# Buffer order in SBUF, column counts of the experts' last groups, and the place of the gate's sums in a fused attention and expert kernel

## The chip, the cores and the metric

The kernel runs on one core of a Trainium2 chip. The metric is the device time of one launch in microseconds; a comparison goes by the median of several runs. The profile is that of one further execution.

## What is computed

Three layers follow each other. Chunked attention works on 8 x 8 heads, 576 rows of 64, in chunks of 64 rows (softmax of q k^T / 8, times v); its output, 4608 tokens of 512, goes through a dense block, x = g @ w_out with h = x @ w_in and g = h - tanh(h) (512 to 2048 to 512). Then a router chooses two of eight experts for each token:

```python
logits = x @ w_gate
noise_scale = np.log1p(np.exp(x @ w_noise))
noisy_logits = logits + noise_scale * noise
top2 = np.argpartition(-noisy_logits, 2, axis=1)[:, :2]
...
h = np.maximum(x[mask] @ w1[e], 0.0)
out[mask] += top2_w[mask, k, None] * (h @ w2[e])
```

Each expert has 512 to 1024 to 512. With the inputs that the reference draws, the eight experts get 1106, 1152, 1151, 1148, 1239, 1151, 1109 and 1160 tokens; these counts come from running the reference's own arithmetic, and the kernel knows them only at run time.

## The kernel before

All products of the dense block and of the experts are made from split float32 numbers: each operand has a high and a low part, and three of the four products of parts are summed (`PASSES`), so a product over 512 inputs is 12 matmuls (3 passes by 4 blocks of 128). A *step* is one block of 128 hidden units: `products1` (L331) makes 12 matmuls into a PSUM bank `hp`, with the weights as the stationary 128 x 128 operand and the tokens (tile `xt0` or `xt1`) as the moving one; `activate` has ScalarE and VectorE turn `hp` into two parts in `gt`; `products2` (L439) sums 3 matmuls of 512 columns into a bank `acc` for each tile of 128 tokens, with `gt` as the stationary operand. TensorE's order is written out by hand: `layer1` of step f, then `layer2` of step f - 1, and so on, with slots between for other work (`advance`). An even slot stands between the two layers, an odd one behind both.

The dense block takes the 36 tiles of tokens in 11 groups of `GS` = 4, 3, 4, 3, 4, 3, 3, 3, 3, 3, 3 tiles, 16 steps (32 slots) each. This document calls them stage 0 to stage 10. In a stage g, the attention of later tiles is done at *visits* (`u_attn`: four transposes into `pt`, 64 small matmuls into `pair`), and the routing of group g - 1 is done in units placed by a list `hs`: `u_lg` (L519, partial logits, copied to `ls`), `u_gate` (L538, sums of the four parts of each logit by a matmul with `summat`), `u_gate2` to `u_gate3` (a chain of small operations on VectorE and ScalarE, and on GpSimd at its end) and `u_pos` (L636, L637). `u_gate` writes to a bank that `misc` hands out of the two banks of `pair`, the same two that the visits use.

The experts come next, three groups of tokens each (`EVEN`, `ODD`): 3 and 4 tiles, or 4 and 3, and a last group that begins at token 896 of the expert's list (c0 = 7) with room for 352. Each has 8 steps. Only in the last group does the count matter: TensorE alone loads it in a register, and `where_filled` (L465) builds each step of that group twice under a branch, for 352 columns (three tiles) and for 256 (two tiles). The last group of the last expert keeps its eight `gt` (here `gl`), and `by_tiles` makes its second layer at the very end, tile by tile. Results are scaled and scattered to the output by `put`.

SBUF tiles come from one pool `sp`; a tile's place in SBUF follows from the order in which the tags first ask for room.

Of the kernel before, what the change touches and what calls it, by code (L numbers as in the profile page):

```python
# [9 lines left out]
F32 = mybir.dt.float32  # L10
F32R = mybir.dt.float32r
# [11 lines left out]
SEAL = 896  # L23
DUMMY = 512
SIZES = None
EVEN = [(0, 4, 512), (4, 3, 384), (7, 3, 352)]
ODD = [(0, 3, 384), (3, 4, 512), (7, 3, 352)]

# [2 lines left out]
def moe_chain_kernel(ctx: ExitStack, tc: tile.TileContext, q, k, v, w_in, w_out, wgn, noise,  # L31
# [3 lines left out]
    NTOK = NT * 128  # L35
    GS = SIZES or [4, 3] * 3 + [3] * ((NT - 21) // 3)
    NG = len(GS)
# [9 lines left out]
    sp = ctx.enter_context(tc.tile_pool(name="sp", bufs=1))  # L47
# [17 lines left out]
    pools = {}  # L65
# [16 lines left out]
    def bank():  # L82
        return pools["pair"][:, after("pair", 2)]

    def misc(*shape):
        n = 1
        for m in shape:
            n *= m
        p = bank()[:, :n]
        return p.rearrange("p (a b) -> p a b", b=shape[1]) if len(shape) > 1 else p  # L90
# [3 lines left out]
    def blk(name, tag, bufs, dt=F32):  # L94
        return sp.tile([128, 512], dt, name=name, tag=tag, bufs=bufs)
# [7 lines left out]
    def spare(tag, f):  # L103
        return raws[tag][f].bitcast(F32)
# [13 lines left out]
    def load_v(i):  # L118
        V[i] = spare("wb", NF1 - 2)[:, i % 2] if 2 <= i < GS[0] else blk("v", "v", 2)
        nc.sync.dma_start(V[i], v[i])  # L120

    PS, MX, PT, PX, LO = {}, {}, {}, {}, {}

# [202 lines left out]
    def products1(s, n):  # L326
        w = s.A[s.f].rearrange("p s (d m) -> p s d m", d=4)
        i = 0
        for a, b in PASSES:
            for d in range(4):  # L330
                nc.tensor.matmul(s.hp[:, :n], lhsT=w[:, a, d, :], rhs=s.xt[:, b, d, :n],  # L331
                                 start=(i == 0), stop=(i == 11))
                i += 1
# [94 lines left out]
    def products2(s, nt, only=None):  # L428
        order = [(i, j) for i in range(3) for j in range(nt)]
        if s.f == s.nf - 1:  # L430
            order.sort(key=lambda t: t[1])
        elif s.kind == 1 and s.g == s.f == 0:
            order.sort(key=lambda t: (0, 2, 1)[t[0]])
        if only:
            order = [t for t in order if t[1] in only]
        for i, j in order:
            a, b = PASSES[i]
            m = s.tiles[j]
            nc.tensor.matmul(s.grp["acc"][j][:m], lhsT=s.gt[:, a, j * 128:j * 128 + m],  # L439
                             rhs=s.B[s.f][:, b, :], start=(s.f == 0 and i == 0),  # L440
                             stop=(s.f == s.nf - 1 and i == 2))
# [13 lines left out]
        products2(s, len(s.tiles))  # L455
        finish(s)

    def where_filled(t, fn):

        nt = len(t.tiles)
        with tc.If(t.count > 128 * (t.c0 + nt - 1)) as c:  # L465
            fn(nt)
        with c.Else():
            fn(nt - 1)


    Y, X2T, LS = {}, {}, {}
    GT = {}
    cum = cp.tile([128, 8], F32, name="cum")
    spacer = cp.tile([1, 1], F32, name="spacer")
# [34 lines left out]
    def u_lg(g):  # L509
        n = GS[g]  # L510
        if g + 1 < NG - 1 and GS[g + 1] < 4:
            p = pools["acc"].tile([128, 512], F32, name="acc", bufs=4)[:, :128 * n]
            p = p.rearrange("p (a b) -> p a b", b=128)
        else:
            p = misc(n, 128)
        for j in range(n):
            x = X2T.pop(G0[g] + j)
            for d in range(4):
                nc.tensor.matmul(p[32 * d:32 * d + 32, j, :], lhsT=wg[:, d, :], rhs=x[:, d, :],  # L519
                                 start=True, stop=True, tile_position=(0, 32 * d))  # L520
        LS[g] = sp.tile([128, 4, 128], F32, name="ls", bufs=1)[:, :n]
        nc.scalar.copy(LS[g], p)

    def small(name, shape, dt=F32, bufs=1):
        return sp.tile(shape, dt, name=name, bufs=bufs)
# [7 lines left out]

    def u_gate(g):
        n, i0 = GS[g], G0[g]
        p = misc(n, 16)
        for j in range(n):
            nc.tensor.matmul(p[:, j, :], lhsT=LS[g][:, j], rhs=summat, start=True, stop=True)  # L538
        lg = small("lg", [128, 4, 16])[:, :n, :]
        nc.scalar.copy(lg, p)  # L540
        t = small("t", [128, 4, 8])[:, :n, :]
        z = lg[:, :, 8:16]
        nc.vector.scalar_tensor_tensor(t, z, -1.0, z, op0=ALU.mult, op1=ALU.min)
        nc.scalar.activation(t, t, AF.Exp)
        GT[g] = lg, t, NZ.pop(g)
# [351 lines left out]
    def advance(s, h):  # L897
        p = prev[0]
        if p and p.held:
            p = None  # L900
        s_tail, p_tail = [t if t and t.count is not None else None for t in (s, p)]
        both = s_tail and p_tail

        def tail1(nt):
            products1(s, min(128 * nt, s.n))

        def tail2(nt):
            products2(p, nt)

        if both:  # L910
            new_hp(s)
            new_acc(p)
            where_filled(s, lambda nt: (tail1(nt), tail2(nt)))
            activate(s)
            finish(p)
        elif s_tail:
            new_hp(s)
            where_filled(s, tail1)
            activate(s)
        elif s:  # L920
            layer1(s)
        for fn in slots[h]:
            fn()
        if s:
            issue(s)
        if p_tail and not both:
            new_acc(p)
            where_filled(p, tail2)
            finish(p)
        elif p and not both:  # L930
            layer2(p)
        for fn in slots[h + 1]:
            fn()
        if s:
            issue(s)
        prev[0] = s
# [54 lines left out]
    p = warm_up(5)  # L991
# [40 lines left out]

    plans = [EVEN, ODD] if NG % 2 == 0 else [ODD, EVEN]
    g0 = plans[0][0]
# [28 lines left out]
    visits = []  # L1063
    at(H1, decoded)
    for g in range(1, NG - 1):
        hs = (1, 5, 9, 14, 18, 23) if g == 1 else (5, 9, 15, 21) if GS[g + 1] > 3 else (9, 14, 20) if GS[g] < 4 else (5, 14, 20)
        for h in hs:
            visits.append((H1 * g + h, n0 if n0 < NT else None))
            n0 += 1
# [8 lines left out]
    for g in range(NG):  # L1078
        h0 = H1 * g
        at(h0, load_nz, g)  # L1080
        if g > 0:
            n = GS[g - 1]
            for j in range(n):
                i = G0[g - 1] + j
                at(h0 + 1 + j, u_z, i)
                at(h0 + 5 + j, u_yt, i)

            if g == NG - 1:
                hs = (9, 11, 12, 13, 15, 17, 17, 19, 20, 23)
            elif g == 1:  # L1090
                hs = (9, 11, 12, 13, 15, 17, 21, 22, 22, 26)
            elif GS[g + 1] > 3:
                hs = (9, 11, 12, 13, 17, 18, 19, 20, 20, 25)
            else:
                hs = (9, 11, 12, 13, 17, 18, 19, 19, 20, 23)
            for h, fn in zip(hs, (u_lg, u_gate, u_gate2, u_gate2h, u_gate2a, u_gate2b, u_gate2m,
                                  u_gate2c, u_gate3, u_pos)):
                at(h0 + h, fn, g - 1)
        if g == 0:
            at(H1 + 6, sums)  # L1100
            at(26, store_consts)
            for o, f in ((0, 3), (1, 2), (1, 3)):
                at(0, fetch_w, o, f)
            for f in range(NF1):
                at(2 * f, fetch_w, 0, f + 4)
                at(2 * f, prep_w, 1, f)
                at(2 * f, decode_w, 0, f + 2)
                at(2 * f, rebias_w, 0, f + 3)
                at(2 * f + 1, fetch_w, 1, f + 4)
                at(2 * f + 1, prep_w, 0, f + 2)  # L1110
                at(2 * f + 1, decode_w, 1, f + 1)
                at(2 * f + 1, rebias_w, 1, f + 2)
        else:
            for f in range(0, NF1):
                if g == 1:
                    if f < E:
                        at(h0 + 2 * f, zero_x, 2 * f)
                        at(h0 + 2 * f, zero_x, 2 * f + 1)
                elif (g - 2) * NF1 + f < NT + DUMMY // 128:
                    at(h0 + 2 * f, zero_out, (g - 2) * NF1 + f)  # L1120
        if g == NG - 1:
            at(h0 - 4, u_cum)
            at(h0 - 2, u_bump)
            at(h0 + 12, load_list0)
            for c in range(min(3, SEAL // 128)):
                at(h0 + 8 + 3 * c, fetch_x, 0, c)
            for c in range(g0[1]):
                at(h0 + min(21 + 4 * c, H1 - 1), first_xt, c)
            for f in range(NF2):
                at(h0 + 2 * f + 7, fetch_e, 0, f)  # L1130
                at(h0 + 2 * f + 10, prep_e, 0, f)
# [52 lines left out]
    for g in range(NG):  # L1184
        grp = {}
        for f in range(NF1):
            s = step1(g, f)
# [4 lines left out]
    for gi, (e, ge, c0, nt, n) in enumerate(groups):  # L1192
        grp = {}
        for f in range(NF2):
            s = Step()
# [64 lines left out]
```

## Time and profile before

| | us |
|---|---|
| median of 3 runs | 1743.22 |
| lowest, highest | 1742.43, 1743.45 |
| profiled execution, whole time | 1742.54 |
| its span, first to last instruction | 1740.5 |
| TensorE (PE) busy in the span | 1728.3 |
| granted TensorE clock, mean | 0.999 |

The whole time of the profiled execution is 2.04 us longer than its span. PE is TensorE's matmul side, PEld its loading of weights, DVE VectorE, ACT ScalarE, POOL GpSimd. Ends of matmuls are modelled and overlap the next, so the rhythm of matmuls is read from the starts of consecutive groups in the timeline.

### The profile page before, as it was taken

How to read it: one execution, taken by the hardware profiler on the slowest of the kernel's cores; microseconds unless marked ns; L12 is line 12 of the kernel's file. 1: busy time of each engine (PE TensorE's matmuls, PEld its weight loads, DVE VectorE, ACT ScalarE, POOL GpSimd, SP SyncE). 2: the span in 40 equal slices, each digit the busy share in tenths (PEclk: the TensorE clock that was granted, in tenths of full speed). 3: DMA queues.
4: the chain of work that ended last, by engine and by line, in shares of the span. 5: the costliest groups of instructions: out<-in, count | busy, mean ns of one | idle time of the engine just before them, and what ended most of it. 6: DMA issues, size and time to landing. Idle time of an engine off the chain costs nothing.

```text
span 1740.5 us, 28351 instructions
## 1 busy us (share of the span) xinstructions
PE 1728.3 (99%) x10776; PEld 1485.9 (85%) x10777; DVE 790.6 (45%) x2070; ACT 547.5 (31%) x1108; POOL 491.7 (28%) x752
## 2 busy tenths in 40 slices
PE   8999999999999999999999999999999999999998
PEld 6788888888888888888898888988898888988887
DVE  8866443644454544544465333434333333343321
ACT  5643322332232333323342323323223222232211
POOL 4640403040304213031253523222232222232112
PEclk9999999999999999999999999999999999999999
DMA  8546525571323222121354543543354353443312
GB/s 315 182 128 161 163 63 155 126 206 43 107 79 113 82 79 101 55 95 38 112 175 120 130 108 79 106 106 68 87 103 104 73 96 85 93 111 71 65 25 37
DMA packets 197830, 184.68 MB, mean 106 GB/s; under 512 B 80176, under 2 KB 139568, under 8 KB 197680
## 3 DMA queue, kind: packets, MB, share of 16 engines
q1 hardware_dynamic: 178064, 142.73, 27.5%
q0 software_dynamic: 19328, 39.41, 11.8%
q8 instruction: 96, 1.57, 0.4%
q14 instruction: 54, 0.44, 0.1%
q10 hardware_dynamic: 288, 0.52, 0.1%
HBM read 118.76 MB, written 63.84 MB: 105 GB/s over the span
## 4 chain that ended last, share of the span: by engine, by line
PE 97%; DVE 1%; ACT 0%; POOL 0%; issue 0%; POOLq 0%; ACTq 0%; DVEq 0%
PE hp L331 47%; PE acc L439 46%; PE pair L136 2%; PE pt L190 1%; PE one L136 0%; PE pair L538 0%; PE acc L519 0%; PE hp L820 0%; DVE sm L172 0%; DVE e L156 0%; PE pair L519 0%; POOL out_dram L794 0%; DVE mx L149 0%; DVE g L370 0%; ACT xt L206 0%
## 5 line engine op out<-in xcount | busy, mean ns | idle before, releaser
L331 PE MATMUL hp<-xt,wa 128*128 128x384 f32 (+3 forms) x4416 | 879.3, 348 | 0.9 <-ACT xt L206 0.9
L439 PE MATMUL acc<-wb,gt 128*128 128x512 f32 x3432 | 859.0, 395 | 0.0
L331 PEld LDWEIGHTS hp<-xt,wa 128*128 128x128 f32 x4416 | 765.2, 188 | 82.9 <-issue 2.6
L439 PEld LDWEIGHTS acc<-wb,gt 128*128 128x128 f32 x3432 | 636.3, 188 | 131.0
L378 DVE SCALAR_TENSOR_TENSOR gt<-hp,gt 128x384 fp32r<-128x384 f32 (+2 forms) x184 | 109.2, 593 | 437.3 <-ACT gt L375 437.3
L375 ACT ACTIVATE gt<-hp 128x384 fp32r<-128x384 f32 (+2 forms) x184 | 95.6, 520 | 445.9 <-PE hp L331 426.0
L370 DVE TENSOR_TENSOR g<-hp,g 128x384 f32<-128x384 f32 (+1 forms) x176 | 104.1, 592 | 249.9 <-ACT g L367 249.3
L367 ACT ACTIVATE g<-hp 128x384 f32<-128x384 f32 (+1 forms) x176 | 91.4, 519 | 335.5 <-PE hp L331 330.8
L316 POOL TENSOR_TENSOR wb<-st,wb 128x512 fp32r<-128x512 f32 x64 | 92.9, 1451 | 321.5 <-ACT wb L314 321.5
L373 DVE TENSOR_TENSOR gt<-g,gt 128x384 fp32r<-128x384 f32 (+1 forms) x160 | 94.1, 588 | 96.0 <-ACT gt L371 95.5
L371 ACT CAST gt<-g 128x384 fp32r<-128x384 f32 (+1 forms) x176 | 95.4, 542 | 130.3 <-DVE g L370 116.2
L794 POOL DMA_INDIRECT out_dram<-o,lsa x73 | 119.3, 1634 | 53.4 <-DVE o L791 31.3
L396 POOL COPY spacer<-mark 1x1 f32<-1x1 f32 x182 | 47.2, 260 | 304.3 <-DVE mark L391 237.8
L613 POOL TENSOR_SCALAR r<-d 128x3 f32<-128x3 f32 (+1 forms) x11 | 3.3, 297 | 425.5 <-ACT d L604 425.4
L664 POOL DMA_INDIRECT xs<-yr,row x72 | 71.2, 988 | 32.0 <-issue 25.1
L269 DVE TENSOR_TENSOR xt<-xg,xt 128x512 fp32r<-128x512 f32 x80 | 54.3, 679 | 54.7 <-ACT xt L268 54.7
L268 ACT CAST xt<-xg 128x512 fp32r<-128x512 f32 x80 | 48.8, 610 | 91.6 <-DVE xg L491 90.1
L664 POOL DMA_INDIRECT lst<-pay,row x72 | 70.2, 975 | 16.1 <-issue 14.0
L491 DVE STREAM_TRANSPOSE xg<-xg 128x512 f32<-128x512 f32 x80 | 56.3, 704 | 0.0
L316 DVE TENSOR_TENSOR wa<-st,wa 128x512 fp32r<-128x512 f32 x64 | 44.1, 688 | 5.5 <-ACT wa L314 5.4
L314 ACT CAST wa<-st 128x512 fp32r<-128x512 f32 x64 | 39.3, 613 | 4.6 <-DMA st<-in_w_dram 4.6
L314 ACT CAST wb<-st 128x512 fp32r<-128x512 f32 x64 | 39.7, 620 | 0.4 <-DMA st<-in_w_dram 0.4
(197 smaller groups left out, 896.3 us busy)
## 6 DMA issues: line engine op xcount, KB each, us to landing
st<-in_w_dram SPq DMA_DIRECT2D x128, 256.0 KB, 2.9
xg<-xs SPq DMA_DIRECT2D x320, 64.0 KB, 2.4
out_dram<-zero SPq DMA_DIRECT2D x40, 256.0 KB, 4.5
x2d<-y SPq DMA_DIRECT2D x36, 256.0 KB, 2.3
z<-x2d SPq DMA_DIRECT2D x144, 64.0 KB, 2.1
yr<-x2d SPq DMA_DIRECT2D x36, 256.0 KB, 4.5
q<-in_q_dram SPq DMA_DIRECT2D x34, 256.0 KB, 4.1
v<-in_v_dram SPq DMA_DIRECT2D x34, 256.0 KB, 3.6
```

Of the source, the lines that this page charges most:

```text
L314: nc.scalar.copy(w[:, 0, :], x)
L316: eng.tensor_tensor(w[:, 1, :], x, w[:, 0, :].bitcast(F32), op=ALU.subtract)
L331: nc.tensor.matmul(s.hp[:, :n], lhsT=w[:, a, d, :], rhs=s.xt[:, b, d, :n], start=(i == 0), stop=(i == 11))
L367: nc.scalar.activation(g, hp[:, :n], AF.Tanh)
L370: nc.vector.tensor_tensor(g, hp[:, :n], g, op=ALU.subtract)
L371: nc.scalar.copy(hi, g)
L373: eng.tensor_tensor(lo, g, hi.bitcast(F32), op=ALU.subtract)
L375: nc.scalar.activation(hi, hp[:, :n], AF.Relu)
L378: nc.vector.scalar_tensor_tensor(lo, hp[:, :n], 0.0, hi.bitcast(F32), op0=ALU.max, op1=ALU.subtract)
L439: nc.tensor.matmul(s.grp["acc"][j][:m], lhsT=s.gt[:, a, j * 128:j * 128 + m], rhs=s.B[s.f][:, b, :], start=(s.f == 0 and i == 0), stop=(s. ...
L664: s = nc.gpsimd.indirect_dma_start(out=to, out_offset=bass.IndirectOffsetOnAxis(ap=at, axis=0), in_=src, in_offset=None)
L794: a = nc.gpsimd.indirect_dma_start(out=out, out_offset=bass.IndirectOffsetOnAxis(ap=en[:m, 0:1], axis=0), in_=o[:m], in_offset=None, compu ...
```

## The change

Two tiles `xt0` and `xt1`, two of `gt`, one of `e` and one of `y` are asked for early, behind the weights' buffers, and are not used: their tags get their room there. `where_filled` chooses among 224, 256, 288 and 352 columns by a tree of two tests; the second layer has as many tiles as the columns need (2, 2, 3, 3). Where only the second layer is left (the last step of a group), the choice stays 256 or 352. In the groups where `u_lg` writes to a spare bank of `acc`, `u_gate` writes to the same bank and no more to `pair`. In stages 3 and 5 to 9, one visit moves to slot 13 (from 15 in stage 3, from 14 in stages 5 to 9), `u_gate` moves from slot 11 to 13, where it stands directly behind that visit, `u_gate2` from 12 to 14 and `u_gate2h` from 13 to 16.

```diff
+CUTS = (224, 256, 288)
...
+    for n, m in ((0, 512), (1, 384)):
+        sp.tile([128, 2, 4, m], F32R, name=f"xt{n}", bufs=1)
+    sp.tile([128, 2, 512], F32R, name="gt", bufs=2)
+    blk("e", "e", 2)
+    blk("y", "y", 4)
...
-    def where_filled(t, fn):
-        nt = len(t.tiles)
-        with tc.If(t.count > 128 * (t.c0 + nt - 1)) as c:
-            fn(nt)
-        with c.Else():
-            fn(nt - 1)
+    def where_filled(t, fn, cuts=CUTS):
+
+        def pick(ns):
+            half = len(ns) // 2
+            if half == 0:
+                return fn(ns[0])
+            with tc.If(t.count > 128 * t.c0 + ns[half - 1]) as c:
+                pick(ns[half:])
+            with c.Else():
+                pick(ns[:half])
+
+        pick([n for n in cuts if n < t.n] + [t.n])
...
     def u_lg(g):
-            p = pools["acc"].tile([128, 512], F32, name="acc", bufs=4)[:, :128 * n]
-            p = p.rearrange("p (a b) -> p a b", b=128)
+            LP[g] = pools["acc"].tile([128, 512], F32, name="acc", bufs=4)
+            p = LP[g][:, :128 * n].rearrange("p (a b) -> p a b", b=128)
...
     def u_gate(g):
-        p = misc(n, 16)
+        if g in LP:
+            p = LP.pop(g)[:, :16 * n].rearrange("p (a b) -> p a b", b=16)
+        else:
+            p = misc(n, 16)
...
-        def tail1(nt):
-            products1(s, min(128 * nt, s.n))
+        def tail1(n):
+            products1(s, n)
-        def tail2(nt):
-            products2(p, nt)
+        def tail2(n):
+            products2(p, (n + 127) // 128)
...
-            where_filled(p, tail2)
+            where_filled(p, tail2, (256,))
...
-        hs = (1, 5, 9, 14, 18, 23) if g == 1 else (5, 9, 15, 21) if GS[g + 1] > 3 else (9, 14, 20) if GS[g] < 4 else (5, 14, 20)
+        hs = (1, 5, 9, 14, 18, 23) if g == 1 else (5, 9, 13, 21) if GS[g + 1] > 3 else (9, 13, 20) if GS[g] < 4 else (5, 14, 20)
...
             elif GS[g + 1] > 3:
-                hs = (9, 11, 12, 13, 17, 18, 19, 20, 20, 25)
+                hs = (9, 13, 14, 16, 17, 18, 19, 20, 20, 25)
+            elif GS[g] < 4:
+                hs = (9, 13, 14, 16, 17, 18, 19, 19, 20, 23)
             else:
                 hs = (9, 11, 12, 13, 17, 18, 19, 19, 20, 23)
```

## Rows read from the trace of the kernel before

**Rows 1.** The page: busy times by engine, and the chain that ended last by line.
```profile
PE 1728.3 (99%) x10776; PEld 1485.9 (85%) x10777; DVE 790.6 (45%) x2070; ACT 547.5 (31%) x1108; POOL 491.7 (28%) x752
...
PE hp L331 47%; PE acc L439 46%; PE pair L136 2%; PE pt L190 1%; PE one L136 0%; PE pair L538 0%; PE acc L519 0%; PE hp L820 0%; DVE sm L172 0%; DVE e L156 0%; PE pair L519 0%; POOL out_dram L794 0%; DVE mx L149 0%; DVE g L370 0%; ACT xt L206 0%
```
**Rows 2.** Groups by form: count, busy us, mean ns, idle before.
```profile
L331 PE MATMUL hp<-xt,wa 128*128 128x256 f32 x576 | 76.6, 282 | 0.0
...
L331 PE MATMUL hp<-xt,wa 128*128 128x352 f32 x192 | 32.3, 322 | 0.0
```
**Rows 3.** Timeline of PE, last group of expert 1: start us, us, instructions.
```profile
1090.90 1.59 PE L331 MATMUL hp<-xt,wa 128*128 128x256 f32 x12
1092.33 1.54 PE L439 MATMUL acc<-wb,gt 128*128 128x512 f32 x6
1093.71 1.60 PE L331 MATMUL hp<-xt,wa 128*128 128x256 f32 x12
```
**Rows 4.** Chain that ended last, from 1680 us: start us, us, what.
```profile
1703.58 13.30 PE hp L331 x84
1716.89 10.98 PE acc L439 x48
```
**Rows 5.** Timeline of PEld around the gate's sums of stage 5.
```profile
567.53 0.64 PEld L538 LDWEIGHTS pair<-summat,ls 128*128 128x128 f32 x5
568.09 0.30 PEld L331 LDWEIGHTS hp<-xt,wa 128*128 128x128 f32 x2
```
**Rows 6.** Timeline of ACT in expert 7's last group, and what it waited for.
```profile
1707.42 0.46 ACT L375 ACTIVATE gl<-hp 128x352 fp32r<-128x352 f32 x1 [1.37 <-PE hp L331]
1709.32 0.46 ACT L375 ACTIVATE gl<-hp 128x352 fp32r<-128x352 f32 x1 [1.44 <-PE hp L331]
```
**Rows 7.** Timeline of DVE there.
```profile
1707.92 0.53 DVE L378 SCALAR_TENSOR_TENSOR gl<-hp,gl 128x352 fp32r<-128x352 f32 x1 [1.37 <-ACT gl L375]
```
**Rows 8.** Branches of the tails: duration min/median/max, first and last start.
```profile
L465 PEldq COMPARE_BRANCH  x88: 65/207/371, 979.8 to 1714.3; - x88
```
**Rows 9.** Timeline of PE at the first tail, expert 0.
```profile
977.41 2.96 PE L331 MATMUL hp<-xt,wa 128*128 128x512 f32 x12
...
983.01 1.59 PE L331 MATMUL hp<-xt,wa 128*128 128x256 f32 x12
...
987.21 1.60 PE L331 MATMUL hp<-xt,wa 128*128 128x256 f32 x12
988.64 1.55 PE L439 MATMUL acc<-wb,gt 128*128 128x512 f32 x6
```
**Rows 10.** The page's DMA queues: packets, MB, share of 16 engines.
```profile
q8 instruction: 96, 1.57, 0.4%
```
**Rows 11.** Timeline of PE, stage 5: the gate's sums, whole steps, the next visit.
```profile
567.53 0.74 PE L538 MATMUL pair<-summat,ls 128*128 128x16 f32 x6
568.12 2.36 PE L331 MATMUL hp<-xt,wa 128*128 128x384 f32 x12
570.31 2.26 PE L439 MATMUL acc<-wb,gt 128*128 128x512 f32 x9
572.41 2.28 PE L331 MATMUL hp<-xt,wa 128*128 128x384 f32 x12
574.52 0.60 PE L190 MATMUL pt<-ident,e 128*128 128x128 f32 x4
```
**Rows 12.** Timeline of ACT, stage 5: the exponent of the gate, and its wait.
```profile
569.82 0.22 ACT L544 ACTIVATE t<-t 128x24 f32<-128x24 f32 x1 [1.31 <-DVE t L543]
```
**Rows 13.** Timeline of PE, stage 4: whole steps of 512 columns.
```profile
436.28 2.95 PE L331 MATMUL hp<-xt,wa 128*128 128x512 f32 x12
439.06 2.95 PE L439 MATMUL acc<-wb,gt 128*128 128x512 f32 x12
```
**Rows 14.** The same in expert 0.
```profile
960.63 2.96 PE L331 MATMUL hp<-xt,wa 128*128 128x512 f32 x12
963.43 2.96 PE L439 MATMUL acc<-wb,gt 128*128 128x512 f32 x12
```

More of the change, by code (lines that the diff above doesn't have):

```diff
@@ L456, in layer2 @@
         finish(s)
-    def where_filled(t, fn):
-        nt = len(t.tiles)
-        with tc.If(t.count > 128 * (t.c0 + nt - 1)) as c:
-            fn(nt)
-        with c.Else():
-            fn(nt - 1)
-    Y, X2T, LS = {}, {}, {}
+    def where_filled(t, fn, cuts=CUTS):
[8 more added lines that the diff above has]
+        pick([n for n in cuts if n < t.n] + [t.n])
+    Y, X2T, LS, LP = {}, {}, {}, {}
     GT = {}
@@ L912, in advance @@
             new_acc(p)
-            where_filled(s, lambda nt: (tail1(nt), tail2(nt)))
+            where_filled(s, lambda n: (tail1(n), tail2(n)))
             activate(s)
```

## The prediction

> **What bounds the kernel now.** I read the page first: busy times and the chain that ended last, then the groups by form, the timeline of PE in the stretches that the diff touches, and last what the other engines do there. The reader is to see that TensorE is busy for 1728.3 of 1740.5 us, that the chain runs on it alone, and that the two products, L331 and L439, hold 93% of the chain [rows 1]. The matmuls of both tails' shapes have no idle time before them [rows 2]. So a saving counts where it shortens TensorE's own stream, and an edit on another engine counts only if TensorE comes to wait for it.
>
> The groups by form also say what the branches chose: 576 matmuls of 256 columns are six experts (8 steps by 12), 192 of 352 columns are two [rows 2]. This agrees with the counts: 1239 and 1160 exceed 1152, the other six do not.
>
> **Part 1, columns by count.** The count less 896 gives the columns needed: 210, 256, 255, 252, 343, 255, 213, 264. Experts 0 and 6 go from 256 columns to 224, expert 7 from 352 to 288; experts 1, 2, 3, 5 stay at 256 and expert 4 at 352. Each step has 12 matmuls and there are 8 steps, so 2 x 96 = 192 matmuls become 32 columns narrower and 96 become 64 narrower. Second layers keep their tiles (2 for 224, 3 for 288), so nothing changes there.
>
> What a column is worth: twelve matmuls of 256 columns take 1092.33 - 1090.90 = 1.43 us, 119 ns each [rows 3]. In expert 7 the first layers of seven steps stand alone: 84 matmuls of 352 columns in 13.30 us, 158 ns each [rows 4]. That is 39 ns for 96 columns, 0.41 ns a column.
>
> *Expert 7*: 288 columns lie between two measured widths, so I interpolate: 158 - 64 x 0.41 = 132 ns, 26 ns saved, times 96: 2.5 us. Bounds: the two ends come from different surroundings, so 24 to 27 ns, 2.3 to 2.6 us. It is paid out in full only if TensorE stays the slowest there. A step shrinks from 1.90 to 1.59 us. A bank of `hp` is used every second step, and before it is free ScalarE (0.46 us, begun at 1707.42) and VectorE (0.53 us, to 1708.45) must have read it; both still process 352 columns. TensorE's next matmul into that bank comes at the end of the following step, 1709.32, where ScalarE's next wait ends [rows 6, 7]. The cover is 0.87 us now and about 0.56 us then. What follows, the last second layers of `by_tiles` from 1716.89 [rows 4], begins with the oldest `gl`, so it moves forward by the whole saving and the end with it.
>
> *Experts 0 and 6*: 224 columns are narrower than anything that the trace shows of this shape. On the straight line they would take 119 - 32 x 0.41 = 106 ns, 13 ns saved, 2.5 us in all. But each matmul has its own loading of 128 x 128 weights, and a row shows how fast loads can follow each other when the moving side is tiny: at the gate's sums, 16 columns wide, five loads in 568.09 - 567.53 = 0.56 us, 112 ns each [rows 5]. I take 112 ns: 7 ns saved, times 192: 1.4 us. Bounds: 0, if 119 ns is already what loads and matmuls make together, and 2.5 us.
>
> The Trainium skill weighs against this part (TensorE: Matmul & The Clock Gate, sections "Back-to-back issue gap" and "LDWEIGHTS (loading the stationary operand)"): a warm matmul follows the last after N / 2.4 + 2.5 ns, and a load of P columns takes P / 1.2 ns whatever else is chosen. As an estimate from that page, 256 columns would take 109.2 ns and 224 no less than the load's 106.7, so 2.5 ns or 0.5 us would be saved instead of 1.4. The row has 119 ns for 256 columns, ten above that figure, and 112 for the loads, five above, so the trace does not follow the page's numbers, but the order of the two is the same.
>
> **Part 2, the branches.** The tails have 88 branch records, 65 ns where a test falls through, about 207 when it jumps, 371 at most [rows 8]. For 224 columns a step will have two jumping tests, for 256 and 288 one of each kind and a jump at the end, for 352 two tests and jumps at the ends; I expect about 190 records. Price on the path: nothing. What hides them is that TensorE's sequencer is ahead of its matmuls: the first branch runs at 979.8, when the matmuls are at the eleventh of the block begun at 977.41, while the block that it guards starts at 983.01 [rows 8, 9]. Between lie one or two matmuls of that block and the 12 of the second layer, some 14 pairs. In a step with 224 columns 14 pairs are 8 x 112 + 6 x 230 ns = 2.3 us (a second layer's six matmuls take 1.38 us [rows 3]), in expert 7's 14 x 132 = 1.8 us; the longest way through a step is three records besides a fall-through, 3 x 0.21 + 0.07 = 0.7 us at most. Without the cover each record that is new in a step would stand in TensorE's stream: one jump for experts 0, 6 and 7 (0.21 us), a jump and a fall-through for the other five (0.27), times 8 steps: 8 x (3 x 0.21 + 5 x 0.27) = 16 us.
>
> **Part 3, the gate's sums.** Where TensorE comes back from other work to the main products, the first block is longer: after the gate's sums it takes 570.31 - 568.12 = 2.19 us, the next one of the same shape 574.52 - 572.41 = 2.11 [rows 11]. The sums themselves (0.59 us) stay. With `u_gate` directly behind a visit, TensorE returns once instead of twice: 0.08 us in each of six stages, 0.5 us. Bounds: 0.2 (if the change from the visit to the sums has a price of its own) and 0.6. Moving the visits by one or two slots removes no instruction of theirs, and their loads of q, k, v go with them, two visits ahead.
>
> What could be late next: ScalarE's exponent for the gate waits for VectorE, 1.31 us already now [rows 12]; behind a visit VectorE has three passes over 512 columns first (0.53 us for 352 columns [rows 7], so some 0.8 each), and the exponent stands about 2 us in ScalarE's queue, ahead of the tanh of the next step. That tanh can't begin before its 2.11 us block of matmuls is done, about when the exponent ends, and the second layer that needs it comes two blocks later. `u_gate2` and `u_gate2h` move behind it by 2 and 3 slots; `u_gate2a` at 17 still follows them. Price nothing. `u_gate` no longer waits for a bank of `pair`; the trace has no such wait to win (the chain gives its line 0%) [rows 1].
>
> **Part 4, the places in SBUF.** No instruction changes. Whether an address costs anything I bound by the two tiles at different addresses: a block of 256 columns takes 988.64 - 987.21 = 1.43 us with `xt1` (expert 0) and 1.43 with `xt0` (expert 1) [rows 3, 9]. Price nothing. There is a small unknown, though: twelve matmuls of 512 columns take 2.78 us in some stretches and 2.80 in others, the same tiles in both [rows 13, 14]. Experts have 8 x 8 x 2 = 128 such blocks, stages 0, 2 and 4 have 96. If edits tip half of these from one rhythm to the other, it is 0.02 x 64 = 1.3 us either way. I take 0 and keep both ends.
>
> **The sum.** 2.5 + 1.4 + 0.5 = 4.4 us. The profiled execution took 1742.54 us, its span 1740.5 and 2.04 around it, and would come to 1738.1. The median of the runs is 0.68 above that execution, so the median becomes 1743.22 - 4.4 = **1738.8**, 0.25% less. About 0.2% (3.5 us, the border at 1739.7) is what a measurement of this kernel tells from no change.
>
> **The rivals.** (a) *224 columns are worth nothing, loads bind already at 256.* For it: the loads' own rhythm is only 7 ns below [rows 5]. Against: it is below. Then 2.5 + 0.5 = 3.0 us are left: 1740.2, within 0.2%. The same end is reached if the rhythm of the 512-column blocks tips the wrong way (4.4 - 1.3 = 3.1). The change would do what it says, and not be seen. (b) *The rhythm tips to the short one or 224 columns follow the straight line*: 4.4 + 1.3 or 4.4 + 1.1, about 1737.6. (c) *Instruction fetch at the jumps, slower.* The program's instructions come in 96 packets of 16 KB, 0.4% of 16 engines' span, which is 0.004 x 16 x 1740 / 96 = 1.2 us each [rows 10]. I take these for TensorE's: 21,553 instructions run [rows 1] and some 2,500 are jumped over, so a packet holds about 250. The change doubles a tail's step from 39 pairs to 78 (first steps from 24 to 48, expert 7's too): 7 x (24 + 7 x 39) + 8 x 24 = 2,271 pairs or 4,500 instructions, 18 packets more. The jumps of a step then skip some 80 to 120 instructions, so they leave their packet in about 28 of the 64 steps. If each then waits for a packet, the jump lasts 1.2 + 0.4 = 1.6 us, still under the lead of 1.8 to 2.3. It decides from a jump of some 2.1 to 2.6 us on, when 28 x 0.28 = 8 us eat the gain; with 0.5 us exposed each it is 14 us lost and 4.4 won, 1752.8. Against: the longest of 88 branches took 0.37 us [rows 8], so none waited for a packet yet.
>
> By the Trainium skill (Runtime: NRT & Kernel Launch, section "Instruction fetch mechanics") a taken branch whose target isn't in the current two-page window stalls for a fetch of the target's page, which speaks for (c); no row here shows such a stall.
>
> **Chances.** Forecast 0.60, (b) 0.10, (a) 0.24, (c) and any other loss 0.06. Faster by over 0.2% are the forecast and (b): 0.70; within 0.2%: 0.24; slower: 0.06. Range: the best case 2.6 + 2.5 + 0.6 + 1.3 = 7.0 us, 1736.2; the least case without (c) 2.3 + 0 + 0.2 - 1.3 = 1.2 us, 1742.0. I cut the last tenth of (a) and give 1736.2 to 1741.8.
>
> **What would show it.** 192 matmuls of 224 columns at about 112 ns, 96 of 288 at 132, expert 7's 84 in 11.1 us instead of 13.30; 384 left at 256 and 96 at 352; branch records doubled with no longer block at a tail's start; some 114 packets of instructions; the L331 block behind the visit and the sums longer once by 0.08 us; whole 512-column blocks still 2.78 or 2.80. The forecast is wrong if TensorE's blocks at unchanged widths change their rhythm over long stretches, if a block starts late behind a branch, or if 224 columns stay at 119 ns.

## The result and the profile after

The median went from 1743.13 us (4 runs, 1742.43 to 1743.45) to 1723.30 us (4 runs, 1721.91 to 1723.60). The ratio is 0.9885, interval 0.9873 to 0.9897: 19.8 us less, where 4.4 were forecast. The direction was right; the time lies outside the range.

The page of the changed kernel: busy times, an instruction queue, the head of the chain that ended last.

```profile
PE 1708.7 (99%) x10776; PEld 1481.0 (86%) x10777; DVE 790.0 (46%) x2070; ACT 547.8 (32%) x1108; POOL 490.7 (29%) x752
...
q8 instruction: 115, 1.88, 0.5%
...
PE 97%; DMA 1%; DVE 1%; issue 1%; SPq 0%; POOL 0%; ACT 0%; POOLq 0%; ACTq 0%; DVEq 0%
```

TensorE still sets the time, with as many instructions as before [rows 1]: 10776 matmuls now take 1708.7 us instead of 1728.3. So the 20 us were not waits. The next view, groups by form, says which matmuls became shorter: count, then busy us, mean ns, idle before.

```profile
L446 PE MATMUL acc<-wb,gt 128*128 128x512 f32 x3408 | 846.1, 393 | 1.2 <-DVE o L802 1.2
L338 PE MATMUL hp<-xt,wa 128*128 128x384 f32 x2304 | 437.5, 338 | 0.0
L338 PE MATMUL hp<-xt,wa 128*128 128x512 f32 x1344 | 324.5, 390 | 1.1 <-ACT xt L213 1.1
L338 PE MATMUL hp<-xt,wa 128*128 128x256 f32 x384 | 51.1, 283 | 0.0
L338 PE MATMUL hp<-xt,wa 128*128 128x224 f32 x192 | 24.0, 274 | 0.0
...
L338 PE MATMUL hp<-xt,wa 128*128 128x352 f32 x96 | 16.7, 323 | 0.0
L338 PE MATMUL hp<-xt,wa 128*128 128x288 f32 x96 | 13.0, 294 | 0.0
```

The tails, where columns went away, fell from 76.6 + 32.3 = 108.9 us [rows 2] to 51.1 + 24.0 + 16.7 + 13.0 = 104.8. The rest came from matmuls that the change doesn't touch: the same view of before has 855.8 us for the 3408 second-layer matmuls, 331.9 for the 1344 of 512 columns and 438.6 for the 2304 of 384; they lost 9.7, 7.4 and 1.1 us (groups overlap at their ends, so the differences don't add up to 19.6 exactly). The timeline of PE in expert 0 shows it block by block (start us, us, instructions):

```profile
951.46 2.88 PE L446 MATMUL acc<-wb,gt 128*128 128x512 f32 x12
954.18 2.88 PE L338 MATMUL hp<-xt,wa 128*128 128x512 f32 x12
956.90 2.88 PE L446 MATMUL acc<-wb,gt 128*128 128x512 f32 x12
```

From start to start a block of twelve takes 2.72 us, 227 ns a matmul; before it took 2.80 here, 233 ns [rows 14]. Neither 2.78 nor 2.80, the two rhythms that the prediction knew, is left.

What differs is where the operands lie. By the program's addresses, before had `xt0` at byte 187520 of each partition and the two `gt` at 203904 and 208000: 128 above a multiple of 512. The weights `wa`, `wb`, which are the other operand of the same matmuls, and `xt1` (212480) start on multiples of 512. In the changed kernel all do: `xt0` 162816, `xt1` 179200, `gt` 191488 and 195584.

### The profile page after: what moved, and what is told of

It is laid out like the page before. It is cut to its first block, busy times and chain, and to the rows that moved or that the text cites. A ratio compares the mean times of both kernels' runs of the same rounds, so it can differ in the third digit from the quotient of the medians.

```text
span 1721.6 us, 28431 instructions
## 1 busy us (share of the span) xinstructions
PE 1708.7 (99%) x10776; PEld 1481.0 (86%) x10777; DVE 790.0 (46%) x2070; ACT 547.8 (32%) x1108; POOL 490.7 (29%) x752
## 4 chain that ended last, share of the span: by engine, by line
PE 97%; DMA 1%; DVE 1%; issue 1%; SPq 0%; POOL 0%; ACT 0%; POOLq 0%; ACTq 0%; DVEq 0%
PE hp L338 46%; PE acc L446 46%; PE pair L143 2%; PE pt L197 1%; PE one L143 0%; DMA st<-in_w_dram 0%; SPq L503 0%; PE acc L527 0%; PE acc L549 0%; PE hp L831 0%; DMA xs<-yr,row 0%; PE pair L527 0%; POOL xs L675 0%; POOL out_dram L805 0%; DVE e L163 0%
## 5 line engine op out<-in xcount | busy, mean ns | idle before, releaser
L338 PE MATMUL hp<-xt,wa 128*128 128x384 f32 (+5 forms) x4416 | 866.8, 345 | 1.1 <-ACT xt L213 1.1
L446 PE MATMUL acc<-wb,gt 128*128 128x512 f32 x3432 | 849.4, 393 | 1.2 <-DVE o L802 1.2
```

## The experiments

Theory: the place of the two operands of a matmul against each other sets the rhythm, and the narrower tails, the sums and the branches give 3 to 5 us. Rivals: the gain belongs to another edit; to the region in SBUF; or to the absolute address. All times are medians, beside 1743.5 us for the kernel before on the same chips (e1 to e12). The rhythms are medians in us a block, from start to start, over blocks that stand between two blocks of the main products (83 first layers of 512 columns, 86 second layers of 12 matmuls, some 150 of 9, some 150 first layers of 384). "+128" means that the tiles begin 128 bytes further than in the changed kernel.

| kernel | time | ratio | first, 512 | second x12 | second x9 | first, 384 |
|---|---|---|---|---|---|---|
| before | 1743.13 | 1 | 2.796 | 2.796 | 2.090 | 2.110 |
| after | 1723.30 | 0.9885 | 2.720 | 2.720 | 2.081 | 2.106 |
| e1 places alone | 1726.35 | 0.9902 | 2.720 | 2.720 | 2.081 | 2.106 |
| e2 all but places | 1740.76 | 0.9984 | 2.796 | 2.796 | 2.090 | 2.110 |
| e3 before, aligned | 1725.44 | 0.9898 | 2.720 | 2.720 | 2.081 | 2.106 |
| e4 tokens and `gt` +128 | 1742.27 | 0.9994 | 2.796 | 2.794 | 2.095 | 2.112 |
| e9 weights +128 too | 1723.53 | 0.9885 | as after | | | |
| e7 tokens and `gt` +256 | 1722.86 | 0.9881 | as after | | | |
| e8 tokens and `gt` +64 | 1736.97 | 0.9960 | 2.765 | 2.799 | 2.097 | 2.083 |
| e5 `gt` +128 | 1736.74 | 0.9964 | 2.757 | 2.796 | 2.090 | 2.110 |
| e6 `xt0`, `xt1` +128 | 1727.93 | 0.9910 | 2.792 | 2.735 | 2.055 | 2.105 |
| e10 `xt1` +128 | 1720.48 | 0.9869 | 2.720 | 2.720 | 2.055 | 2.105 |
| e11 as e10, 384 columns in `xt0` +128 | 1719.00 | 0.9863 | 2.720 | 2.720 | 2.055 | 2.105 |

**Which part.** e1 is the kernel before with the five early lines alone, e2 the changed kernel without them.

```diff
# e1: before, and these; e2: after, without these
+    for n, m in ((0, 512), (1, 384)):
+        sp.tile([128, 2, 4, m], F32R, name=f"xt{n}", bufs=1)
+    sp.tile([128, 2, 512], F32R, name="gt", bufs=2)
+    blk("e", "e", 2)
+    blk("y", "y", 4)
```

> The kernel before with the early asking for xt0, xt1, gt, e and y alone. Theory (the place of xt0 and gt in SBUF sets the rhythm of the main matmuls): whole blocks of 12 matmuls of 512 columns go from 2.80 to 2.72 us, nine of 512 from 2.09 to 2.08, and the time falls by 14 to 17 us to about 1728. Rival (the rhythm tips because of what is done between the blocks, the moved gate and the narrower tails, and the place is of no account): blocks stay at 2.78 to 2.80 us and the time at 1743.

> The changed kernel without the early asking: columns by count and the moved gate alone. Theory (place): the three terms of the prediction's sum and no more, 1743.1 - 4.5 = 1738.6, with blocks of 512 columns at 2.78 to 2.80 us. Rival (work between the blocks tips the rhythm): 1723, blocks at 2.72 us.

e1 took 1726.35 us (ratio 0.9885 to 0.9918), e2 1740.76 (0.9975 to 0.9994). The two parts, 17.2 and 2.8 us below 1743.5, make 20.0 beside the 19.8 of both: they add up, and the places carry six sevenths.

**Which property of the place.** e3 is the kernel before with two small tags of 384 bytes, which stand behind `gt` there, asked for ahead of `xt0`. All of it stays in its region; `xt0` goes to 187904, `gt` to 204288 and 208384, and `xt1`, `e` and `y` stay where they were.

```diff
# e3
+    sp.tile([1, 1], F32, name="mark", bufs=4)
+    sp.tile([128, 4, 8], F32, name="nz", bufs=2)
     p_mm(0)
     p_hi(0)
```

> The kernel before; two small tags (mark and nz, 384 bytes of a partition) get their room just before xt0, so that xt0 and gt move up by 384 bytes and begin at multiples of 512 bytes as the weights do, in the same region as before. Theory (the offset against a multiple of 512 counts): most of the gain of the early asking, about 1728, blocks at 2.72 us. Rival (the region counts, beside the weights or far from them): unchanged, 1743.

It took 1725.44 us (0.9881 to 0.9914). Its timeline of PE, expert 0:

```profile
955.26 2.88 PE L439 MATMUL acc<-wb,gt 128*128 128x512 f32 x12
957.98 2.88 PE L331 MATMUL hp<-xt,wa 128*128 128x512 f32 x12
960.70 2.88 PE L439 MATMUL acc<-wb,gt 128*128 128x512 f32 x12
```

The lines are those of rows 14, in the same program but for the addresses, with 2.72 us in place of 2.80. The rival of the region falls, and `e` and `y`, which did not move, have no part in it.

e4 puts the same tiles of the changed kernel 128 bytes further; e9 does so with the weights as well, by a constant ahead of everything; e7 takes 256 bytes, e8 64.

```diff
# e4, ahead of the early lines      (e7: "nz", [128, 4, 8]; e8: "mx", [128, 2, 4, 1])
+    sp.tile([1, 1], F32, name="mark", bufs=4)
# e9, behind the constant spacer; the early lines stay as they are
+    cp.tile([128, 32], F32, name="shift")
```

> The changed kernel with the tag mark (128 bytes) asked for just before the early tiles, so that xt0, xt1, gt, e and y begin 128 bytes past a multiple of 512 while the weights stay on one. Theory (offset): the gain of the place is lost, about 1739, blocks of 512 columns at about 2.80 us. Rival (region): 1723, blocks at 2.72 us.

> The changed kernel with a constant of 128 bytes more ahead of everything, so that the weights wa and wb as well as xt0, xt1 and gt begin 128 bytes past a multiple of 512. Theory (the offset of one operand against the other counts): as the changed kernel, 1723, blocks of 512 columns at 2.72 us. Rival (the absolute multiple of 512 counts): 1740 or more, blocks at 2.80 us.

> The changed kernel with the tag nz (256 bytes) asked for ahead of the early tiles, so that xt0, xt1 and gt begin 256 bytes past a multiple of 512. Theory (a multiple of 512 is what counts): the gain of the place is lost, about 1740, blocks 2.79 us. Rival (a multiple of 256 is enough): 1723, blocks 2.72 us.

> The changed kernel with xt0, xt1 and gt 64 bytes past a multiple of 256, the weights on one. Theory (any offset that isn't a multiple of 256 spoils the rhythm alike): blocks of 512 columns at 2.79 to 2.80 us, 1740. Rival (the loss grows with the offset): about half of it, 1731.

e4 gave 19.0 of the 19.8 us back (0.9985 to 1.0004), e9 none (0.9856 to 0.9913): the place of one operand against the other counts, not the absolute address. e7 lost nothing (0.9852 to 0.9910), so 256 bytes are as good as 0; the multiple of 512 that the theory named was wrong. e8 lost 13.7 us (0.9944 to 0.9976), 69% of the gain, more than its rival's half and less than the theory's whole, and not in all shapes: its groups by form have

```profile
L447 PE MATMUL acc<-wb,gt 128*128 128x512 f32 x3408 | 857.8, 396 | 1.3 <-DVE o L803 1.3
L339 PE MATMUL hp<-xt,wa 128*128 128x384 f32 x2304 | 434.0, 337 | 0.0
L339 PE MATMUL hp<-xt,wa 128*128 128x512 f32 x1344 | 330.1, 395 | 1.2 <-ACT xt L214 1.2
```

The second layers are slower than even before (855.8), but the 384-column matmuls are 3.5 us faster than with everything aligned (437.5). So "aligned is fast, the rest slow" is too simple.

**Which tile.** e5 leaves `xt0`, `xt1` aligned and moves `gt` (with `e` and `y`); e6 moves `xt0` and `xt1` and aligns `gt` again.

```diff
# e5, between xt1 and gt
+    sp.tile([1, 1], F32, name="mark", bufs=4)
# e6, ahead of xt0, and then between xt1 and gt
+    sp.tile([1, 1], F32, name="mark", bufs=4)
...
+    sp.tile([128, 4, 8], F32, name="nz", bufs=2)
+    sp.tile([128, 2, 4, 1], F32, name="mx", bufs=2)
+    sp.tile([128, 8, 1], F32, name="sm", bufs=2)
```

> The changed kernel with gt (and e and y behind it) 128 bytes past a multiple of 512, xt0 and xt1 left on one. Theory (each product pays for its own pair of operands, the one that is loaded against the one that streams): second layers of 12 matmuls at 2.80 us and of nine at 2.09, first layers still 2.72, the time about half way, 1731. Rival (one tile off the multiple spoils both products): both at 2.80, 1739 to 1742.

> The changed kernel with xt0 and xt1 128 bytes past a multiple of 512 and gt on one. Theory (own pair): first layers of 12 matmuls of 512 columns at 2.80 us, second layers 2.72, about 1731. Rival (one tile spoils both): both 2.80, 1739 to 1742.

e5 lost 13.4 us (0.9944 to 0.9983), e6 4.6 (0.9881 to 0.9939); together 18.0, near e4's 19.0. Timelines of PE in expert 0, first e5, then e6:

```profile
952.53 2.92 PE L339 MATMUL hp<-xt,wa 128*128 128x512 f32 x12
955.29 2.96 PE L447 MATMUL acc<-wb,gt 128*128 128x512 f32 x12
958.09 2.92 PE L339 MATMUL hp<-xt,wa 128*128 128x512 f32 x12
```

```profile
954.59 2.95 PE L342 MATMUL hp<-xt,wa 128*128 128x512 f32 x12
957.38 2.90 PE L450 MATMUL acc<-wb,gt 128*128 128x512 f32 x12
960.12 2.96 PE L342 MATMUL hp<-xt,wa 128*128 128x512 f32 x12
```

With `gt` off, the second layer takes the whole 2.80 us and the first 2.76; with `xt0` off it is the first layer that takes 2.79 to 2.80 and the second 2.73. At 512 columns each product follows mainly its own pair of operands, and its neighbour changes too: by half of its own loss in e5 (2.757), by a fifth in e6 (2.735). It counts for the stationary operand (`gt` in the second layer) as for the moving one (`xt0` in the first). Neither time was the expected 1731: e5 also slowed the first layers, and e6 won some 5 us back in blocks of another shape (192 x 0.026, an estimate from the table).

e6 showed one thing more: second layers of nine matmuls fell to 2.055 us, below the aligned 2.081. There the first layer beside them has 384 columns, and their own pair (`gt` and `wb`) is aligned as before. Two kernels follow this up. e10 moves `xt1` alone; e11 also lets 384-column groups that use `xt0` begin 128 bytes inside it.

```diff
# e10: xt0 first, then
+    sp.tile([1, 1], F32, name="mark", bufs=4)
     sp.tile([128, 2, 4, 384], F32R, name="xt1", bufs=1)
+    sp.tile([128, 2, 4, 1], F32, name="mx", bufs=2)
+    sp.tile([128, 8, 1], F32, name="sm", bufs=2)
# e11: that, and in new_xt
-        return sp.tile([128, 2, 4, m], F32R, name=f"xt{par % 2}", bufs=1)
+        x = sp.tile([128, 2, 4, m], F32R, name=f"xt{par % 2}", bufs=1)
+        return x[:, :, :, 32:416] if (m, n) == (512, 384) else x
```

> The changed kernel with xt1 alone 128 bytes past a multiple of 256 (xt0, gt and the weights on one). Where both xt tiles stood so, second layers of nine matmuls took 2.055 us instead of 2.081 and first layers of 384 columns were unchanged. Theory (the second layer's blocks inherit that rhythm from the first layer of the same step, so xt1 alone brings it to the groups that use xt1): 144 steps of three tiles use xt1, 144 x 0.026 = 3.7 us less than the changed kernel, about 1719.5. Rival (it takes both tiles, or the rhythm depends on neighbouring groups): 1723.

> As the kernel with xt1 alone past a multiple, and groups of three tiles of 384 columns that lie in xt0 (stages 6, 8, 10) use its columns 32 to 415, so they too begin 128 bytes past a multiple. Theory (the offset of what streams against what is loaded counts, wherever the tile begins): 48 more steps at 2.055 us, another 1.2 us, about 1718.3. Rival: no further change.

Timeline of PE in e11, expert 7's second group:

```profile
1660.65 2.27 PE L342 MATMUL hp<-xt,wa 128*128 128x384 f32 x12
1662.75 2.22 PE L450 MATMUL acc<-wb,gt 128*128 128x512 f32 x9
1664.81 2.27 PE L342 MATMUL hp<-xt,wa 128*128 128x384 f32 x12
```

1720.48 us (0.9852 to 0.9885) and 1719.00 (0.9846 to 0.9879). A step of three tiles takes 2.10 + 2.06 = 4.16 us. e11 is the fastest kernel here, 4.3 us under the changed one. The runs of e10 and e11 overlap, but in their traces stages 6, 8 and 10, the ones that e11 touches, are 0.31, 0.31 and 0.34 us shorter. So a 384-column tile is better 128 bytes off the weights' alignment, a 512-column tile on it.

**The branches.** In e12 only the last expert's last group chooses among four widths; the others go back to 256 or 352.

```diff
-            where_filled(s, lambda n: (tail1(n), tail2(n)))
+            where_filled(s, lambda n: (tail1(n), tail2(n)), (256,))
...
-            where_filled(s, tail1)
+            where_filled(s, tail1, CUTS if s.held else (256,))
```

> The changed kernel with the four-way choice only in the last expert's last group; all other tails choose between 352 and 256 as before. Experts 0 and 6 give back their narrower columns (0.75 us each by the profiles). Theory (the volume of instructions jumped over costs: packets fetched behind jumps and beside the weights' loads): the wait at expert 0's tail (1.4 us) and the branches of 0.5 to 3 us are gone up to the last group, time 1723.2 + 1.5 - 1.6 = about the same, 1723. Rival (those waits come from faster steps, not from the instructions): they stay, 1724.8.

It took 1723.26 us (0.9868 to 0.9901), the time of the changed kernel, with two of three narrowed tails given up. Branches of the tails, duration ns min/median/max, first the changed kernel and then e12:

```profile
L471 PEldq COMPARE_BRANCH  x184: 65/196/2408, 972.8 to 1696.1; - x184
```

```profile
L471 PEldq COMPARE_BRANCH  x96: 65/207/578, 972.2 to 1695.5; - x96
```

With the choices go the long branches, and expert 0's tail no longer waits as it does in the changed kernel (next section).

## Why the prediction failed, step by step

**Part 4 is the step that failed**: "Whether an address costs anything I bound by the two tiles at different addresses ... Price nothing", with 1.3 us either way. It carries 17.2 us (e1). The comparison took a width that hardly shows the cost: before, a block of 256 columns takes 1.437 us with `xt0`, which was off, and 1.433 with `xt1`, which was aligned (medians of all such experts). At 512 columns the same places make 2.796 and 2.720. The bound also knew only the two rhythms of the trace, 2.78 and 2.80, and took them for the ends, though every block of 512 columns but the last 48 matmuls ran with one operand off. Rival (b), the rhythm that tips short, had the direction and a thirteenth of the size. A hint was shown: the last second layers, whose `gl` stand in rooms of the weights and so on their alignment, took 10.98 / 48 = 229 ns [rows 4], where the same shape with `gt` took 2.80 / 12 = 233 [rows 14]; they still take 10.98 us after the change (below). The sizes agree: a group of expert steps at 512 columns has 16 blocks, 16 x 0.076 = 1.22 us, and expert 0's lost 1.10, the eight together 9.3; stages 0, 2 and 4 lost 1.4, 1.7 and 1.9; 2 to 3 us are left for the groups of three tiles (differences of the first blocks' start times in the two traces). The bound had a slip too: half of its 128 + 96 blocks are 112, not 64, and 2.2 us instead of 1.3, which would have made the range 0.9 us wider at either end.

**Part 1, columns.** Expert 7 as forecast: the chain that ended last has

```profile
1686.99 11.06 PE hp L338 x84
1698.05 10.98 PE acc L446 x48
```

11.06 / 84 = 132 ns as interpolated; the whole tail gave 2.57 us against 2.5. Expert 6, in the timeline of PE:

```profile
1593.20 1.49 PE L338 MATMUL hp<-xt,wa 128*128 128x224 f32 x12
1594.53 1.56 PE L446 MATMUL acc<-wb,gt 128*128 128x512 f32 x6
1595.92 1.49 PE L338 MATMUL hp<-xt,wa 128*128 128x224 f32 x12
```

1.33 us for twelve, 111 ns where 112 was assumed from the loads' rhythm, and 0.77 us for the tail against 0.7. Rival (a), that 224 columns are worth nothing, falls: the step from 256 to 224 is 119 - 111 = 8 ns. So does the estimate of 2.5 ns that was worked out from the Trainium skill (TensorE: Matmul & The Clock Gate, sections "Back-to-back issue gap" and "LDWEIGHTS (loading the stationary operand)"); its first term is a gap that, by the same page, leaves the loads of weights out.

Expert 0's tail, though, grew by 0.9 us instead of shrinking by 0.7. Its timeline, PE first and then, in the view of all engines, what PE waited for:

```profile
980.02 1.49 PE L338 MATMUL hp<-xt,wa 128*128 128x224 f32 x12
982.73 1.63 PE L446 MATMUL acc<-wb,gt 128*128 128x512 f32 x6 [1.21 <-DVE o L802]
984.19 1.49 PE L338 MATMUL hp<-xt,wa 128*128 128x224 f32 x12
```

```profile
979.33 0.62 ACT L321 CAST wa<-st 128x512 fp32r<-128x512 f32 x1 [3.35 <-DMA st<-in_w_dram]
...
981.25 1.26 ACT L800 ACTIVATE o<-acc,ls 128x512 f32<-128x512 f32 x2
...
982.50 0.74 DVE L802 TENSOR_SCALAR o<-acc,ls 128x512 f32<-128x512 f32 x1
```

Read from the bottom: the second layer needs a bank of `acc` that DVE (L802) empties together with ACT (L800); ACT's part stands behind casts of weights, and these waited 3.35 us for a load `st`. From 980.02 the first layer's 1.33 us end at 981.35, the second layer starts at 982.73: 1.4 us lost. In e12 it is 0.1. The DMA views of this stretch, the changed kernel and then e1 (KB each, median us to landing):

```profile
st<-in_w_dram SPq DMA_DIRECT2D x2, 256.0 KB, 3.8
```

```profile
st<-in_w_dram SPq DMA_DIRECT2D x2, 256.0 KB, 2.8
```

That packets of instructions share the queues at that moment and delay `st` is argued, not shown; e12 takes the longer program and the narrower columns away together, but a block that is 0.1 us longer can't cover 1.4. Neither narrower columns nor the choice brings the wait everywhere: expert 6 has both, without it. In the groups by form, every kernel here with the four widths in expert 0 has idle time before second layers put down to DVE's `o`, 0.6 to 1.3 us; before, e1, e3 and e12 have none.

**Part 2, branches at nothing**, held on TensorE's own stream in the changed kernel, but its reason (no branch waits for instructions) failed, and that little was lost is luck. 184 records came (some 190 forecast) and 115 packets (some 114). But the longest branch went from 0.37 us [rows 8] to 2.4 in the changed kernel and to 3.7 in e5: the stall of rival (c) exists. The Trainium skill's rule for it (Runtime: NRT & Kernel Launch, section "Instruction fetch mechanics"), for which no row of before spoke, agrees with these records: the 2.4 us branch, begun at 990.00, has a 16 KB packet of instructions on its way from 990.02 to 990.89. In the changed kernel 0.2 us came through. In e2, e4, e5 and e7 to e10, which have the same branches, eight blocks start 0.2 to 1.4 us late, each by what its branch took beyond 2.3 to 2.4 us. That is the lead of TensorE's sequencer over its matmuls, within the prediction's 2.1 to 2.6, and the changed kernel's longest branch just reaches it. First the branch of e5 in expert 2, whose columns did not change (begun at 1198.26), then its timeline of PE:

```profile
L472 PEldq COMPARE_BRANCH  x184: 65/196/3747, 977.1 to 1709.0; - x184
```

```profile
1199.44 1.55 PE L447 MATMUL acc<-wb,gt 128*128 128x512 f32 x6
1202.19 1.69 PE L339 MATMUL hp<-xt,wa 128*128 128x256 f32 x12 [1.21 <-issue]
```

The second layer's six matmuls are over 1.39 us after 1199.44; the next block comes 1.36 us later. If expert 0's wait belongs to the longer program too, the four-way choice costs 1 to 3.4 us in every kernel here that has it in all experts (an estimate from the start times of the tails of experts 0 and 2).

**Part 3, the gate's sums**: 0.5 us came, but by luck and not from its place. (Rows 5, 11 and 12 are from stage 6, which begins at 539.8 us, and not from stage 5.) Timeline of PE, stage 7 of the changed kernel:

```profile
642.39 0.84 PE L549 MATMUL acc<-summat,ls 128*128 128x16 f32 x6
643.08 2.33 PE L338 MATMUL hp<-xt,wa 128*128 128x384 f32 x12
645.24 2.24 PE L446 MATMUL acc<-wb,gt 128*128 128x512 f32 x9
647.33 2.27 PE L338 MATMUL hp<-xt,wa 128*128 128x384 f32 x12
```

Behind a visit the sums take 643.08 - 642.39 = 0.69 us where they took 0.59 [rows 11]; the second return to the main products that was saved (0.08) is spent on this. The prediction had named it as the lower bound's reason. By start times e2 gains 0.47 us in stage 5 alone and nothing in stages 3 and 6 to 9. Stage 5 had a wait that no term named: before, the second of the two matmuls of `u_pos` waited for GpSimd and began 0.49 us after the first, at 522.40 (first line below); in the changed kernel it follows after 0.04 us (second and third).

```profile
522.89 0.18 PE L637 MATMUL pair<-mk,ones 128*128 128x32 bf16 x1 [0.29 <-POOL mk L628]
```

```profile
518.33 0.19 PE L647 MATMUL pair<-mk,lower 128*128 128x32 bf16 x1
518.37 0.18 PE L648 MATMUL pair<-mk,ones 128*128 128x32 bf16 x1
```

Why the chain of small operations ends earlier there is not shown.

So without Part 4 the edits are worth 2.8 us (e2) where 4.4 were forecast: 2.4 from expert 7, 0.8 from expert 6, 0.5 from stage 5, and 1.1 lost in expert 0 make 2.6 in its trace. The first main matmul also starts up to 1.9 us earlier or later from one profile to the next (1.4 later in the changed kernel and 1.2 in e2 than before); that is not explained.

## What to carry to other kernels

Where matmuls are back to back, look up the byte offsets of both operands modulo 256 early: moving two small tiles of 384 bytes to another place in the order was worth 18 us here (e3), more than all edits of the work itself. Which offset is best depends on the shape, so try it: tiles of 512 columns were best aligned with the weights, tiles of 384 columns 128 bytes off. A change that only reorders allocations is not free by default, and its price is to be bounded at the shape that fills the time, not at a smaller one. Count the paths that a branch adds as instructions to be fetched: the choice paid for itself where the saving was 26 ns a matmul, and in sum not where it was 8 (e12).

## What the runs showed of the hardware

- Twelve matmuls of 512 columns from split float32 take 2.72 us when both operands' starts are 0 or 256 bytes apart (modulo 512) and 2.80 when they are 128 apart (227 and 233 ns each); moving both by 128 changes nothing. At 64 apart first layers take 2.77, second layers 2.80, but 384-column blocks 2.083 instead of 2.106. Other widths differ in sign: lone first layers of 352 columns take 1.93 us aligned (e1, e3) and 1.90 at 128 apart (before), of 288 columns 1.58 and 1.60 (the changed kernel, e2).
- Nine-matmul second layers beside 384-column first layers take 2.055 us when only the first layer's tokens are 128 off, 2.081 when all agree, 2.090 when `gt` is off. Why is open: the runs show which offsets, not what in the chip they disturb.
- Matmuls of 224 columns, each with its own 128 x 128 weights, follow each other every 111 ns, at every offset tried.
- Branches over longer code took up to 2.4 us (3.7 in e5) where the longest was 0.37. A branch made TensorE's matmuls late only where it took more than some 2.3 to 2.4 us.
